# Moving masks, state updates and copies among the steps of a fused attention and feed-forward kernel

## The chip, the cores and the metric

The kernel runs on one core of one Trainium2 chip. The metric is the device time of one execution, in microseconds (us). The engines are TensorE (PE, matmuls; PEld is its weight load), VectorE (DVE), ScalarE (ACT), GpSimd (POOL) and SyncE (SP, which issues the DMAs here). Each engine works through its own list of instructions in the order written and waits for others on semaphores.

## The reference

The input goes through decaying linear attention, and the result through a feed-forward layer with a squared ReLU:

```python
for b in range(nb):                                   # blocks of 64 positions
    intra = np.einsum('bhic,bhjc->bhij', qb, kb) * Dmask[None]
    intra = np.einsum('bhij,bhjd->bhid', intra, vb)
    inter = np.einsum('bhid,bhde->bhie', qb * lam_pow[None], kv_state)
    out[:, :, sl] = intra + inter
    kv_state = lam_block[None, :, None, None] * kv_state + np.einsum('bhsd,bhse->bhde', kb_dec, vb)
x = attn.transpose(0, 2, 1, 3).reshape(B * S, H * D)  # 3072 tokens x 512
h = x @ w_in                                          # 512 x 2048
r = np.maximum(h, 0.0)
return (r * r) @ w_out                                # 2048 x 512
```

Batch 4, 8 heads, 768 positions, head size 64, all in float32.

## The kernel before

Tokens are cut into 24 chunks t of 128 (six per batch entry), each of two blocks of 64. Four chunks make a slice m of 512 tokens, so there are six slices. The feed-forward layer is done per slice in 16 steps f of 128 hidden features: `hidden(m, f)` makes h in PSUM by 12 matmuls of 512 columns (weights and inputs are split into a high and a low part, `wh`/`wl` and `xh`/`xl`, and three products are added), ACT takes the ReLU (`positive`) and squares it twice (`gh`, then h itself), DVE makes the low part (`rest`, tile `gl`), and `project` adds 12 more matmuls into four accumulators. PE's order is: hidden of step f, then the projection of step f-1.

The change lies in the loop of slice 0 (`m == 0`), the first of these passes. Three other things are done beside its 16 steps.

*Weights.* The weights come in as raw words in NLOT = 17 pieces u. Step f works on u = f + 2. `wload` sends for the raw words by DMA, `first` on ACT takes the absolute value (L210, tile A) and scales the low word (L215), DVE does `clamp` (L223), `shift` (L227), `sign` (L234) and `rounded` (L240), ACT writes `wh` by `upper` (L246) and DVE `wl` by `lower` (L249). Step f's hidden needs piece f. There are two A tiles, so `first` of piece u waits for `lower` of piece u-2. POOL's `turn` (L256) follows each `lower`. Below, clamp(3) means the clamp of piece 3.

*Attention of slice 1.* Chunks 4 to 7 are worked on here, and chunk 8 is begun. In steps 2, 6, 10 and 14 (`step == 2`) PE does a `burst` behind hidden: the scores of chunk t+1, the result of chunk t, and the key-value products ("news") of t+1, all in 64x64 matmuls (L386). It uses a PSUM tile y from the pool of h (two tiles, taken in turn) and two banks `b` from the pool `ps_b`. `keep` copies the result out (`xh`, `xl`; L454, L300), `masked` multiplies the scores by the decay mask into tile a (L484; for chunk 4, whose scores come from `look`, L477). The state is carried by `fade(t, b)`, which writes fd times the state before to the state behind, on ACT, four instructions (L514), and `advance(t, b)`, which adds the news of block b to it on DVE (L300, tile st). So advance(t, 0) needs fade(t, 0), and fade(t, 1) reads the state that advance(t, 0) wrote. POOL makes `prep_k` (L471) and `prep_q` (L466, tile qs), ACT the copies `copy_qx` (L169) and `copy_vx` (L164).

*Banks.* Chunk 4's scores and news are made by `look` at the end of step 0, in the two-bank tile `att` of the pool `ps_a`. At the start of step 2 `middle.close()` gives up that pool, and `ps_b` is opened on the same side of PSUM, so its two banks are the ones that `att` had. The framework lets the first matmul into them wait for the last reader of `att`.

The order of each engine's list is the order in which Python calls these functions; there is no scheduler. SP's DMAs too are issued in the order written, and one that waits for a buffer holds up those behind it.

Of the kernel before, what the change touches and what calls it, by code (L numbers as in the profile page):

```python
# [26 lines left out]
G = 4  # L27
# [15 lines left out]
def body(ctx: ExitStack, tc: tile.TileContext, qT, kT, kvq, lam, w, out):  # L43
# [118 lines left out]
    def copy_vx(t):  # L162
        for y, r in enumerate(rows):
            nc.scalar.copy(chunk[t]["vx"][r], chunk[t]["v"][rows[1 - y], 2 * y : 2 * y + 2])  # L164
# [16 lines left out]
    def pieces(u):  # L181
        return slice(max(2 * u - 1, 0), min(2 * u + 1, 2 * NF))
# [3 lines left out]
    def wload(u):  # L186
        nonlocal hole
        if u < NLOT:
            x = pieces(u)
            n = (x.stop - x.start) * DM  # L190
            if u and u % 3 == 0:
                raw[u] = sets[1]
            elif u == 0:
                x_ = wk.tile([P, 2 * DM], I64, name="raw", tag="raw")
                raw[u] = x_[:, 0:DM]
                hole = x_[:, DM : 2 * DM].bitcast(F32)
            else:
                raw[u] = wk.tile([P, n], I64, name="raw", tag="raw")
            for i, j in enumerate(range(x.start, x.stop)):
                of = (1, j // 2 - 1) if j and j % 2 == 0 else (1, NF - 1) if j == 2 * NF - 1 else (0, (j + 1) // 2)  # L200
                nc.sync.dma_start(out=raw[u][:, i * DM : (i + 1) * DM], in_=w[of[0], :, of[1]])
# [43 lines left out]
    def upper(u):  # L245
        nc.scalar.copy(flat(wh, u), cv[u][2].bitcast(F32))  # L246
# [59 lines left out]
    b_, t_, u_, c_, d_, af = (sq[:, i, 0 : NS - 1] for i in range(6))  # L306
# [166 lines left out]
    def masked(t):  # L473
        a = a_of[t] = a_last[0] if t >= G else wk.tile([P, 2, 2, 2, L], F32, name="a", tag="a")
        x, w_ = sc_of.pop(t), mask.rearrange("p j a i -> p j (a i)")
        if t <= G:
            V.tensor_tensor(  # L477
                out=a.rearrange("p j b a i -> p j b (a i)"),
                in0=x.rearrange("p j (b n) -> p j b n", b=2),
                in1=w_.unsqueeze(2).broadcast_to([P, 2, 2, 2 * L]), op=ALU.mult,  # L480
            )
            return
        for j in range(2):
            V.tensor_tensor(  # L484
                out=a[:, j].rearrange("p b a i -> p b (a i)"),
                in0=x[j].rearrange("p (b n) -> p b n", b=2),
                in1=w_[:, j].unsqueeze(1).broadcast_to([P, 2, 2 * L]), op=ALU.mult,
            )

    def before_block(n):  # L490
        return st[:, n % 3]
# [17 lines left out]
    def fade(t, b):  # L509
        n = 2 * t + b  # L510
        if n % (2 * NCB) and b < len(u_of[t]):
            old, new = (before_block(k).rearrange("p a j d -> p (a j) d") for k in (n, n + 1))
            for g in range(4):
                nc.scalar.activation(new[:, g], old[:, g], AF.Identity, scale=fd[:, g : g + 1])  # L514

    def advance(t, b):
        if b < len(u_of[t]):
            n = 2 * t + b
            new = before_block(n + 1).rearrange("p a j d -> p (a j d)")
            if n % (2 * NCB):  # L520
                add(new, u_of[t][b], new)
            else:
                V.tensor_copy(new, u_of[t][b])
        if b:
            del u_of[t]
# [67 lines left out]
    def positive(h):  # L593
        nc.scalar.activation(h, h, AF.Relu)  # L594
# [207 lines left out]
    def new_x(m):  # L802
        xs_of[m] = [wk.tile([P, KT, N], F32R, name=n, tag=n) for n in ("xh", "xl")]
# [98 lines left out]
    for m in range(PLAIN):  # L902
        if m == 0:
            new_x(1)
        else:
            held += [
                wk.tile([P, KT, N], F32, name=f"held{k}", tag=n) for k, n in enumerate(("xh", "xl"))
            ]
        for f in range(NF):
            h = hidden(m, f, *xs_of[m])  # L910
            if m == 0:
                t = G + f // 4
                step = f % 4
                u_ = f + 2
                if step == 2:
                    if f == 2:
                        middle.close()
                        ps_b = ctx.enter_context(
                            tc.tile_pool(name="ps_b", bufs=1, side="right", space=PSUM)
                        )  # L920
                    upper(u_ - 1)
                    x = burst(t + 1, True, True, lambda: positive(h))
                if f == 1:
                    load_kq(t + 1)
                    load_v(t + 1)
                if f == 1:
                    masked(t)
                    advance(t, 0)
                if u_ < NLOT:
                    if f:  # L930
                        clamp(u_)
                    if f == 1:
                        upper(u_ - 1)
                        lower(u_ - 1)
                    if f:
                        shift(u_)
                    sign(u_)
                if f > 1:
                    if step != 2:
                        upper(u_ - 1)  # L940
                    lower(u_ - 1)
                if f:
                    turn(u_ - 1)
                if step == 2:
                    prep_q(t + 1)
                    if t + 1 < 2 * G:
                        load_vx(t + 1)
                    load_kq(t + 2)
                    load_v(t + 2)
                    if t + 1 == 2 * G:  # L950
                        load_kq(t + 3)
                if f == 1:
                    fade(t, 1)
                    advance(t, 1)
                if step == 3:
                    fade(t + 1, 0)
                    masked(t + 1)
                    advance(t + 1, 0)
                if step == 0 and f:
                    fade(t, 1)  # L960
                    advance(t, 1)
                if f == 0:
                    positive(h)
                if f == 0 or step == 2:
                    rest(m, f, h, square(h))
                if u_ < NLOT:
                    rounded(u_)
                    wload(u_ + 3)
                if step == 1 or f == NF - 1:
                    prep_k(t + 1 if step == 1 else t + 2)  # L970
                if f and step != 2:
                    positive(h)
                    rest(m, f, h, square(h))
                if f == 1:
                    copy_qx(t)
                if step == 2:
                    keep(t, x)
                    if t + 1 == 2 * G:
                        copy_vx(t + 1)
                    copy_qx(t + 1)  # L980
                if f == NF - 1:
                    fade(t + 1, 1)
                    advance(t + 1, 1)
                if u_ + 1 < NLOT:
                    first(u_ + 1)
                if prev is not None:
                    project(*prev)
                if f == 0:
                    look(t)
                    fade(t, 0)  # L990
            else:
                t = 2 * G + 1 + f
                if f < 2 * G:
                    x = burst(t, True, True, lambda: positive(h))
                    rest(m, f, h, square(h))
                    keep(t - 1, x)
                    masked(t)
                    state(t)
                    if t + 1 < SOLO:
                        load_v(t + 1)  # L1000
                    prep_q(t)
                    if t + 2 < SOLO:
                        load_kq(t + 2)
                    if t + 1 < SOLO:
                        prep_k(t + 1)
                    copy_vx(t)
                else:
                    squared(m, f, h)
                if f - 1 in SUMS:
                    w_parts(SUMS.index(f - 1), S)  # L1010
                if f in SUMS:
                    S = w_sums(SUMS.index(f))
                if f < 2 * G:
                    copy_qx(t)
                if f == 2 * G + 1:
                    fetch(0)
                    fetch(1)
                if f > 2 * G:
                    x_sums(f - 2 * G - 1)
                    x_parts(f - 2 * G - 1)  # L1020
                project(*prev)
            prev = (m, f)
# [4 lines left out]
    for d in range((NM - PLAIN) // 2):  # L1027
        m1, m2 = PLAIN + 2 * d, PLAIN + 2 * d + 1
        last = d == (NM - PLAIN) // 2 - 1
        for i in range(NPAIR):  # L1030
            t = (PLAIN + 2) * G + i
# [93 lines left out]
```

## Time and profile before

| | us |
|---|---|
| runs, median of 3 (lowest to highest) | 589.23 (588.75 to 589.60) |
| the profiled execution | 588.08 |
| its span, first to last instruction | 586.2 |
| PE busy | 572.8 |
| DVE busy | 323.1 |
| ACT busy | 317.5 |

The profiled execution took 588.08 us, of which the span is 586.2; 1.9 us lie around it. A row of the time lines further below reads: start in us, length in us, engine, line, operation, tile written and tiles read, shapes, count of instructions merged, and in brackets the idle time of the engine just before with what ended it. A length of several merged instructions runs from the first start to the last end, and neighbours on one engine overlap by about 0.1 us. The pass over slice 0 runs from 26 to 130 us.

### The profile page before, as it was taken

Reading aid. Unit: us, or ns where it says so; the run is one execution under the profiler, and the core shown is the slowest. Engines: PE = TensorE matmul, PEld = TensorE weight load, DVE = VectorE, ACT = ScalarE, POOL = GpSimd, SP = SyncE. Lnnn points to the kernel's source line nnn. Section 1 sums busy time; section 2 is a strip of 40 time slices with the busy share of each in tenths; the row PEclk is TensorE's granted clock in tenths of the full one; section 3 lists DMA queues with packets and bytes.
Section 4 is the critical chain, followed back from the end, with each engine's and each line's share of the span. In section 5 each row is a group of like instructions: output and inputs, shape, how many; then the busy total and the mean of one; then the engine's idle time right before and its main releaser. Section 6 shows DMA issues by size and latency. Waiting matters only on the chain.

```text
span 586.2 us, 12793 instructions
## 1 busy us (share of the span) xinstructions
PE 572.8 (98%) x5240; PEld 470.1 (80%) x5240; DVE 323.1 (55%) x587; ACT 317.5 (54%) x594; POOL 66.7 (11%) x87
## 2 busy tenths in 40 slices
PE   8899999999999999999999999999999999999997
PEld 5777887788888888888888888888888888888885
DVE  6899999975767776534344343446433333334222
ACT  3698887976665465445545445634344444444221
POOL 7401202033232000011111101000000000000000
PEclk8999999999999999999999999999999999999999
DMA  8676667346797933856554553300354444411001
GB/s 335 220 283 228 223 217 229 104 128 196 243 364 260 348 130 103 284 164 197 168 166 137 179 173 98 126 1 0 102 168 126 125 122 120 122 50 73 1 0 72
DMA packets 52089, 93.62 MB, mean 160 GB/s; under 512 B 4672, under 2 KB 19520, under 8 KB 52032
## 3 DMA queue, kind: packets, MB, share of 16 engines
q1 hardware_dynamic: 52032, 92.82, 49.5%
q8 instruction: 41, 0.67, 0.4%
q14 instruction: 16, 0.13, 0.1%
HBM read 71.83 MB, written 20.97 MB: 158 GB/s over the span
## 4 chain that ended last, share of the span: by engine, by line
PE 87%; DVE 6%; ACT 3%; issue 2%; DMA 1%; POOL 1%; POOLq 0%; DVEq 0%
PE h L729 26%; PE acc L623 14%; PE acc L628 14%; PE acc L624 13%; PE h L587 11%; PE h L386 4%; PE b L386 3%; DVE A L234 1%; PE att L79 1%; DVE wl L249 1%; DVE A L240 1%; ACT A L210 1%; DVE A L227 1%; DVE A L223 1%; DVE st L500 1%
## 5 line engine op out<-in xcount | busy, mean ns | idle before, releaser
L623 PE MATMUL acc<-wh,gh 128*128 128x512 f32 x384 | 151.7, 395 | 0.0
L624 PE MATMUL acc<-wl,gh 128*128 128x512 f32 x384 | 149.6, 389 | 0.0
L628 PE MATMUL acc<-wh,gl 128*128 128x512 f32 x384 | 149.3, 390 | 0.1
L623 PEld LDWEIGHTS acc<-wh,gh 128*128 128x128 f32 x384 | 72.1, 188 | 16.0 <-issue 0.3
L628 PEld LDWEIGHTS acc<-wh,gl 128*128 128x128 f32 x384 | 72.1, 188 | 15.2
L624 PEld LDWEIGHTS acc<-wl,gh 128*128 128x128 f32 x384 | 72.1, 188 | 14.4
L608 DVE TENSOR_TENSOR gl<-h,gh 128x512 fp32r<-128x512 f32 x48 | 33.1, 689 | 69.7 <-ACT h L603 69.7
L594 ACT ACTIVATE h<-h 128x512 f32<-128x512 f32 x48 | 28.1, 584 | 69.7 <-PE h L587 36.0
L300 DVE TENSOR_TENSOR temp<-h,temp 128x512 f32<-128x512 f32 x48 | 33.0, 688 | 56.9 <-PE h L729 46.8
L729 PE MATMUL h<-wh,ring 128*128 128x512 f32 x224 | 60.0, 390 | 0.0
L594 ACT ACTIVATE temp<-temp 128x512 f32<-128x512 f32 x16 | 10.1, 632 | 88.6 <-DVE temp L300 88.6
L729 PEld LDWEIGHTS h<-wh,ring 128*128 128x128 f32 x224 | 42.0, 188 | 8.9 <-DVE r L300 0.3
L466 POOL TENSOR_TENSOR qs<-set,qpow 128x512 f32<-128x512 f32 (+1 forms) x21 | 26.5, 1260 | 170.7 <-PE b L386 159.2
L587 PE MATMUL h<-xh,wh 128*128 128x512 f32 x128 | 34.6, 392 | 3.0 <-DVE a L484 2.2
L300 DVE TENSOR_TENSOR r<-h,temp 128x512 f32<-128x512 f32 x24 | 16.6, 692 | 34.2 <-PE h L729 33.1
L608 DVE TENSOR_TENSOR gl<-r,gh 128x512 fp32r<-128x512 f32 x24 | 16.6, 690 | 32.9 <-ACT gh L761 32.9
L729 PE MATMUL h<-wl,ring 128*128 128x512 f32 x112 | 34.5, 389 | 0.0
L587 PE MATMUL h<-xh,wl 128*128 128x512 f32 x128 | 34.5, 391 | 0.0
L587 PE MATMUL h<-xl,wh 128*128 128x512 f32 x128 | 34.3, 389 | 0.0
L761 ACT CAST gh<-r 128x512 fp32r<-128x512 f32 x24 | 14.9, 621 | 30.0 <-PE acc L624 30.0
L587 PEld LDWEIGHTS h<-xh,wh 128*128 128x128 f32 x128 | 23.7, 188 | 9.0 <-ACT gh L598 3.0
L729 PE MATMUL h<-wh 128*128 128x512 f32 x112 | 30.1, 390 | 0.0
(180 smaller groups left out, 1040.1 us busy)
## 6 DMA issues: line engine op xcount, KB each, us to landing
ring<-wd SPq DMA_DIRECT2D x56, 256.0 KB, 2.9
raw<-in_w SPq DMA_DIRECT2D x22, 512.0 KB, 4.7
set<-in_kvq SPq DMA_DIRECT2D x19, 512.0 KB, 3.8
wd<-hl SPq DMA_DIRECT2D x16, 512.0 KB, 5.0
wh<-wd SPq DMA_DIRECT2D x28, 256.0 KB, 2.9
wl<-wd SPq DMA_DIRECT2D x28, 256.0 KB, 2.8
set<-in_kT SPq DMA_DIRECT2D x22, 256.0 KB, 4.2
set<-in_w SPq DMA_DIRECT2D x10, 512.0 KB, 4.9
```

Of the source, the lines that this page charges most:

```text
L79: nc.tensor.matmul(w_[:, 0], st[:, 0, 0].rearrange("p a b -> p (a b)"), st[:, 0:2].rearrange("p n c a b -> p (n c a b)"), start=True, stop ...
L300: lambda o, x, y, op=op: V.tensor_tensor(out=o, in0=x, in1=y, op=op)
L386: nc.tensor.matmul(self.banks[row][rows[col], at : at + D], lhsT, rhs, start=key not in self.begun, stop=stop, skip_group_check=True,)
L466: nc.gpsimd.tensor_tensor(out=z, in0=x, in1=w_, op=ALU.mult)
L587: nc.tensor.matmul(h, wt[:, w_in(f), kt * P : (kt + 1) * P], x[:, kt], start=k == 0, stop=k == 11)
L594: nc.scalar.activation(h, h, AF.Relu)
L608: V.tensor_tensor(out=gl, in0=r, in1=gh.bitcast(F32), op=ALU.subtract)
L623: nc.tensor.matmul(accs[m][i], gh[:, cs], wh[:, j], start=f == 0, stop=False)
L624: nc.tensor.matmul(accs[m][i], gh[:, cs], wl[:, j], start=False, stop=False)
L628: nc.tensor.matmul(accs[m][i], gl[:, cs], wh[:, j], start=False, stop=end)
L729: nc.tensor.matmul(bank, w[:, kw * HALF + kt * P : kw * HALF + (kt + 1) * P], x_slot(2 * c + kt, kx), start=first and q == 0, stop=q == 5, ...
L761: nc.scalar.copy(gh, r_of[f])
```

## The change

Five things are written elsewhere in the loop of slice 0. No instruction is added or removed.

- `masked(t+1)` moves from step 3 (behind `fade(t+1, 0)`) to step 2, right behind `keep`.
- At f == 1, `wload(5)` stands behind the loads of chunk 5; before it was called at the end of step 0, ahead of them.
- `advance(4, 0)` moves from behind `masked(4)` to just ahead of `fade(4, 1)`, and `advance(4, 1)` from f == 1 to f == 2.
- `copy_qx(t+1)` moves from step 2 to the end of step 3, `copy_vx(8)` from f == 14 to f == 15.

```diff
                 if f == 1:
                     load_kq(t + 1)
                     load_v(t + 1)
-                if f == 1:
+                    wload(u_ + 2)
                     masked(t)
-                    advance(t, 0)
...
                 if f == 1:
+                    advance(t, 0)
                     fade(t, 1)
+                if f == 2:
                     advance(t, 1)
                 if step == 3:
                     fade(t + 1, 0)
-                    masked(t + 1)
                     advance(t + 1, 0)
...
                     rounded(u_)
-                    wload(u_ + 3)
+                    if f:
+                        wload(u_ + 3)
...
                 if step == 2:
                     keep(t, x)
-                    if t + 1 == 2 * G:
-                        copy_vx(t + 1)
+                    masked(t + 1)
+                if step == 3:
                     copy_qx(t + 1)
                 if f == NF - 1:
+                    copy_vx(t + 1)
                     fade(t + 1, 1)
                     advance(t + 1, 1)
```

DVE's list at the start of step 1, before (-) and now (+). `att` is the tile of `look`, `a<-att,mask` is `masked(4)`, `st<-att,st` an advance of chunk 4, L223 a clamp, L249 the `lower` and L240 the `rounded` of a weight piece:

```order
 L240 ISA A<-raw,A 128x2048
 L477 TENSOR_TENSOR a<-att,mask 128x512
-L300 TENSOR_TENSOR st<-att,st 128x256
 L223 TENSOR_SCALAR A<-A 128x1024
 L249 TENSOR_TENSOR wl<-A,wh 128x1024
```

An advance has left the place behind the mask. The other one of step 1, behind `sign(3)`, is untouched in the list but is now block 0's instead of block 1's. DVE's list in step 2, where `gl<-h,gh` is the low part of h and `xl` that of `keep`:

```order
 L234 SCALAR_TENSOR_TENSOR A<-raw,A 128x1024
 L249 TENSOR_TENSOR wl<-A,wh 128x1024
+L300 TENSOR_TENSOR st<-att,st 128x256
 L608 TENSOR_TENSOR gl<-h,gh 128x512
 L240 ISA A<-raw,A 128x2048
 L300 TENSOR_TENSOR xl<-h,xh 128x2x128
```

Block 1's advance is the new row, behind `lower(3)` of step 2.

ACT's list in step 1 and the start of step 2 now (it has the same rows before, except that the third waits for an earlier DVE instruction and the last for one more). The first four-fold L514 is fade(4, 0), the next two rows fade(4, 1); `L246` is `upper`, `L594`, `L598` and `L603` are the ReLU and the squares of h, `L210` is the start of the next weight piece:

```order
L514 ACTIVATE st<-st,fd 128x64 x4
L246 CAST wh<-A 128x1024 [waits DVE_49]
L514 ACTIVATE st<-st,fd 128x64 [waits DVE_49,Activation_49]
L514 ACTIVATE st<-st,fd 128x64 [waits Activation_49] x3
L594 ACTIVATE h<-h 128x512 [waits PE_49]
L598 ACTIVATE gh<-h 128x512 [waits Activation_49]
L603 ACTIVATE h<-h 128x512
L169 COPY qx<-qs 64x256 [waits Pool_49]
L169 COPY qx<-qs 64x256
L210 ACTIVATE A<-raw 128x1024 [waits DMAHW5_49,DMAHW4_49]
```

No row of these moved; what moved is the DVE instruction for which the third row, the start of fade(4, 1), waits: advance(4, 0).

PE's list at the burst of step 2, before:

```order
L587 MATMUL h<-xh,wl 128x512 x3
L587 MATMUL h<-xl,wh 128x512 x4
L386 MATMUL h<-set_92 64x64 [waits DMAHW1_49,DMAHW0_49,DVE_49]
L386 MATMUL b_777<-set_92 64x64 [waits PE_49]
L386 MATMUL h<-set_92 64x64
```

and now:

```order
L587 MATMUL h<-xh,wl 128x512 x3
L587 MATMUL h<-xl,wh 128x512 x4
L386 MATMUL h<-set_92 64x64 [waits DMAHW7_49,DMAHW6_49,DVE_49]
L386 MATMUL b_776<-set_92 64x64 [waits DVE_49,PE_49]
L386 MATMUL h<-set_92 64x64
```

The order of the matmuls is the same; the first one into a `b` bank has a wait for DVE that it did not have. The banks are those of `att`, and the last reader of `att` is now advance(4, 1), which stands in step 2.

## Rows read from the trace of the kernel before

**Rows 1.** The page's first part: engine, busy us (share of the span), instructions.

```profile
span 586.2 us, 12793 instructions
PE 572.8 (98%) x5240; PEld 470.1 (80%) x5240; DVE 323.1 (55%) x587; ACT 317.5 (54%) x594; POOL 66.7 (11%) x87
```

**Rows 2.** Busy time of each engine in a stretch of the pass over slice 0: stretch, then PE, PEld, DVE, ACT and POOL busy us (instructions), granted clock of PE, DMA share, GB/s.

```profile
60.00:80.00 20.00, 20.00 (x207) 16.39 (x205) 19.70 (x24) 16.25 (x26) 4.10 (x6) 1.00 0.67 219
```

**Rows 3.** Who waited for whom in the stretch 24 to 130 us: us in total, times, longest us.

```profile
ACT qx L169 <- POOL qs L466: 6.2, 4, 2.0
...
DVE A L223 <- ACT A L210: 0.8, 3, 0.3
```

**Rows 4.** PE's time line: the starts of the burst of step 2 and of the projection behind it, the first and the last hidden matmuls of step 3, and the first of steps 4, 5, 6 and 12.

```profile
43.88 0.27 PE L386 MATMUL h<-set 64*64 64x64 f32 x1 [1.32 <-DVE gl L608]
...
45.90 0.50 PE L623 MATMUL acc<-wh,gh 128*128 128x512 f32 x1
...
48.77 1.07 PE L587 MATMUL h<-xh,wh 128*128 128x512 f32 x4
...
50.81 0.84 PE L587 MATMUL h<-xl,wh 128*128 128x512 f32 x3
...
55.77 1.15 PE L587 MATMUL h<-xh,wh 128*128 128x512 f32 x4 [1.40 <-DVE a L484]
...
61.29 1.07 PE L587 MATMUL h<-xh,wh 128*128 128x512 f32 x4
...
66.73 1.07 PE L587 MATMUL h<-xh,wh 128*128 128x512 f32 x4
...
105.76 1.17 PE L587 MATMUL h<-xh,wh 128*128 128x512 f32 x4 [0.84 <-DVE a L484]
```

**Rows 5.** DVE's time line in step 1: mask of chunk 4, its two additions to the state (37.67 and 41.67), the weight pieces 2 and 3 between them, gl of step 1, and `clamp(4)`, the first of step 2.

```profile
36.35 0.68 DVE L477 TENSOR_TENSOR a<-att,mask 128x512 f32<-128x512 f32 x1
37.67 0.42 DVE L300 TENSOR_TENSOR st<-att,st 128x256 f32<-128x256 f32 x1 [0.63 <-ACT st L514]
38.01 0.68 DVE L223 TENSOR_SCALAR A<-A 128x1024 f32<-128x1024 f32 x1
38.61 1.23 DVE L249 TENSOR_TENSOR wl<-A,wh 128x1024 fp32r<-128x1024 f32 x1
39.75 0.69 DVE L227 TENSOR_SCALAR A<-A 128x1024 uint32<-128x1024 uint32 x1
40.53 1.22 DVE L234 SCALAR_TENSOR_TENSOR A<-set,A 128x1024 uint32<-128x1024 uint32 x1
41.67 0.41 DVE L300 TENSOR_TENSOR st<-att,st 128x256 f32<-128x256 f32 x1
...
43.14 0.68 DVE L608 TENSOR_TENSOR gl<-h,gh 128x512 fp32r<-128x512 f32 x1
43.74 1.01 DVE L223 TENSOR_SCALAR A<-A 128x1024 f32<-128x1024 f32 x1
```

**Rows 6.** ACT's time line in step 1: `upper(2)`, fade(4, 1), the ReLU of h of step 1, the copy of qx, `first(4)` and `upper(3)`.

```profile
37.53 1.05 ACT L246 CAST wh<-A 128x1024 fp32r<-128x1024 f32 x1
38.47 1.08 ACT L514 ACTIVATE st<-st,fd 128x64 f32<-128x64 f32 x4
39.43 0.59 ACT L594 ACTIVATE h<-h 128x512 f32<-128x512 f32 x1
...
40.55 0.59 ACT L603 ACTIVATE h<-h 128x512 f32<-128x512 f32 x1
41.17 0.83 ACT L169 COPY qx<-qs 64x256 f32<-64x256 f32 x2
42.03 1.15 ACT L210 ACTIVATE A<-raw 128x1024 f32<-128x1024 f32 x1
...
44.10 1.03 ACT L246 CAST wh<-A 128x1024 fp32r<-128x1024 f32 x1
```

**Rows 7.** DVE's time line of a plain step (4): `clamp(6)` and, three instructions on, `lower(5)`; and `lower(14)` of step 13 with the PE matmuls of step 14 that read its `wl`.

```profile
57.93 0.69 DVE L223 TENSOR_SCALAR A<-A 128x1024 f32<-128x1024 f32 x1
...
60.52 1.22 DVE L249 TENSOR_TENSOR wl<-A,wh 128x1024 fp32r<-128x1024 f32 x1
...
116.31 1.22 DVE L249 TENSOR_TENSOR wl<-A,wh 128x1024 fp32r<-128x1024 f32 x1
...
117.67 1.11 PE L587 MATMUL h<-xh,wl 128*128 128x512 f32 x4
```

**Rows 8.** The granted clock: four stretches as in rows 2 (the clock is the last column but two; 1.00 is 2.4 GHz, 0.50 is 1.2 GHz), the last matmuls of the program, and the same 27 narrow matmuls of the opening at the lower and at the higher clock.

```profile
10.60:14.00 3.40, 2.92 (x90) 2.78 (x86) 1.63 (x5) 1.94 (x8) 3.20 (x4) 0.50 1.02 419
14.00:17.42 3.42, 2.97 (x107) 2.81 (x105) 2.45 (x12) 2.11 (x7) 3.42 (x4) 0.50 0.82 330
17.42:20.85 3.43, 2.82 (x151) 2.41 (x143) 2.62 (x10) 3.32 (x7) 0.85 (x1) 1.00 0.80 274
...
584.05:586.20 2.15, 0.00 (x0) 0.00 (x0) 0.00 (x0) 0.00 (x0) 0.00 (x0) 0.50 0.27 102
...
581.38 0.61 PE L628 MATMUL acc<-wh,gl 128*128 128x512 f32 x2
...
12.18 1.02 PE L386 MATMUL h<-set 64*64 64x64 f32 x27 [0.48 <-DVE mask L355]
...
21.73 0.63 PE L386 MATMUL h<-lent 64*64 64x64 f32 x27 [0.38 <-DVE st L500]
```

## The prediction

> **What bounds the kernel now.** The page's first part comes first [rows 1]: PE is busy for 572.8 of 586.2 us, so an end moves only when PE idles more or less. The table by stretches [rows 2] says why PE idles at all in the pass over slice 0: in 20 us there DVE works 19.70 us and PE 20.00, while ACT works 16.25 and POOL 4.10. Two engines are full at once, and either one's delay is soon the other's. The waits [rows 3] show the only gaps in DVE's chain that belong to this change: ACT waits 6.2 us in four places for POOL's qs before it copies qx, and DVE then waits for A behind it, three times, 0.3 us at most. PE's time line [rows 4] shows what the masks cost: step 4 begins 1.40 us late and step 12 0.84 us late, each waiting for a L484, because the PSUM tile of the burst is not free until its scores are masked. These 2.2 us are what the change can win at most by its first part. Then I read DVE's and ACT's lists in step 1 [rows 5, 6], since that is where the two additions to the state were moved.
>
> **Masks and copies.** `masked(t+1)` goes ahead of clamp, shift, sign and lower, so PE's 1.40 and 0.84 us go; but the two L484 (about 0.34 us each from start to start) now stand ahead of `lower`, so wl of the next step comes 0.7 us later, and DVE, which is full, sets the pace: nothing is won unless DVE idles less. That it does: with `copy_qx` out of step 2, `first` no longer stands behind POOL's qs. Of the three waits of DVE for A in rows 3, one of 0.3 us lies in step 11 and is won; a smaller gap in step 7 I put at 0.1 us, an estimate. Together 0.4 us. `copy_qx` and `copy_vx` are the same instructions on ACT in another place; beyond step 2 ACT has 3.75 us of idle time in 20 [rows 2], which hides them, except in step 3 (below). `wload(5)` behind the loads of chunk 5 waits for the same buffer as before (free once `rounded(2)` ends, just ahead of the mask at 36.35 [rows 5]), and chunk 5 comes sooner on SP. I cost this at nothing: raw piece 5 is first read behind the burst of step 2, at 43.88 at the earliest, and by the sum below far later, so a microsecond more on SP's queue would not be seen.
>
> **The first hold-up: fade(4, 1).** Before, advance(4, 0) runs at 37.67, right behind the mask, and fade(4, 1) starts on ACT at 38.47 as soon as `upper(2)` lets it [rows 5, 6]. Now the DVE list is mask, clamp(3), lower(2), shift(3), sign(3), advance(4, 0). DVE gains nothing by the addition that left: lower(2) needs `upper(2)`, which ends at 37.53 + 1.05 = 38.58, so it starts at 38.6 as before and the addition stands at 41.67, where the other one stood, and ends at 42.08. fade(4, 1) reads what it writes, so it starts at 42.12 instead of 38.47, 3.65 us later, and ACT's list behind it waits: ReLU and squares of step 1, copy_qx(4), first(4). From fade's start to ACT's ReLU are 0.96 us, to the end of the last square 40.55 + 0.59 - 38.47 = 2.67, to first(4) 3.56, to `upper(3)` 5.63 [rows 6]. Hence the square ends at 44.79, gl of step 1 runs on DVE at 44.83 instead of 43.14 and ends at 45.51, A(4) is there at 42.12 + 3.56 + 1.15 = 46.83.
>
> **The second hold-up: the banks of `att`.** The burst of step 2 writes the banks that `att` held, and the last reader of `att` is now advance(4, 1), which stands in DVE's list behind lower(3) of step 2. That addition needs A(4): clamp(4) at 46.87, lower(3) 2.59 us behind it (57.93 to 60.52 in a plain step [rows 7]) at 49.46, the next instruction 1.14 us on (38.61 to 39.75 [rows 5]) at 50.60, its end 0.41 later at 51.01. PE's first burst matmul into a bank follows at 51.07 (0.06 us, as from 43.82 to 43.88 [rows 4, 5]) instead of 43.88: **7.19 us later**. Queued behind it on PE are the whole burst, the projection of step 1 and hidden of step 3; ACT's `mark` and the squares of step 2 wait for the burst's scores.
>
> **The clock.** PE has then idled since hidden of step 2 ended, at 43.88 - 1.32 = 42.56 [rows 4], for 8.5 us but for one narrow matmul. In this trace the granted clock fell to 0.50 at 584.05, 2.06 us after the last matmuls ended (581.38 + 0.61), and in the opening it was at 0.50 from 10.60 to 17.42, while only narrow matmuls ran, and at 1.00 behind them [rows 8]. So I expect the burst to start at 1.2 GHz. At that clock 27 narrow matmuls took 1.02 us, against 0.63 at the higher [rows 8], 1.62 times; the burst's 45.90 - 43.88 = 2.02 us become 3.27, 1.25 more. If the lower clock lasts through the burst alone, that is all; if it lasts 6.8 us from the burst's start (as the opening's low stretch, 10.60 to 17.42), the 3.55 us behind the burst are wide matmuls at half speed and cost 1.78 more, 3.03 in all; if it doesn't fall, nothing. I take 1.6, near the first (the burst and 0.7 us behind it, which costs 0.35), since the row at 14.00 to 17.42 shows that work much like the burst was followed by the higher clock. The Trainium skill (TensorE: Matmul & The Clock Gate, "HAM oscillation — how this bites in real kernels") tells of a kernel whose matmul groups each start at half the clock because PE idles for a transfer between them; this trace agrees in its last rows, where PE's idling ends at 0.50. By that rule alone the sum would be the one below, and a clock that holds would contradict it.
>
> **The sum.** Hidden of step 3 starts 48.77 - 43.88 = 4.89 us behind the burst's start, plus 1.6: at 57.56 instead of 48.77. Its h is done 50.81 + 0.84 - 48.77 = 2.88 us on, at 60.44. ACT then needs 41.17 - 39.43 = 1.74 us for ReLU and squares, 0.86 for the qx that now stands there, and 1.15 for A(6), with 0.04 us of handing over on either side [rows 6]: clamp(6) at 64.27, against 57.93 [rows 7]. That is 6.3 us. From here on DVE is full as before, does the same work to lower(14), and gains the 0.4 us of the copies, so lower(14) ends 5.9 us later than 116.31 + 1.22 = 117.53. PE's step 14 took its wl at 117.67 before, right behind it, and does so again (PE alone would be there sooner: from 57.56 on, eleven steps of 66.73 - 61.29 = 5.44 us and two bursts of 2.02 [rows 4] end at 121.4, while step 14 then starts at 117.67 - 0.91 + 5.9 = 122.7, with the four matmuls ahead of the wl ones at 5.44/24 us each). Behind step 14 DVE has little to do and PE never waits, so the 5.9 us stay to the end. The profiled execution took 588.08; with 5.9 it is 594.0. That execution lies 1.15 us below the median of the runs shown, so on the median I forecast 589.23 + 5.9 = **595.1 us**.
>
> **Rivals** (times on the median).
> - *The clock holds at 2.4 GHz* (its price is then 0 instead of 1.6). For it: PE idled at 1.00 too, as for 0.38 us ahead of the matmuls at 21.73 [rows 8], and 1.32 us ahead of this very burst [rows 4], and the clock stayed. Against it: this gap is eight us long. Step 3 starts at 55.96, clamp(6) 4.7 us late, less 0.4: +4.3, 593.5.
> - *The banks don't hold the burst* (second hold-up absent, first one there). Then the burst starts at 45.57, behind gl of step 1; hidden of step 3 waits for gl of step 2, which stands behind advance(4, 1) and ends at about 51.6; DVE is 2.4 us late at clamp(6): +2.0, 591.2. Against it: the list of PE now has the wait for DVE at exactly that matmul.
> - *The lower clock lasts longer than the opening's*, by 4 us, which costs 2 more than the 3.03: 1.25 + 1.78 + 2 in place of the 1.6, so +9.3, 598.5. For it: in the opening the first low row, 90 narrow matmuls, was not followed by the higher clock [rows 8]. Against it: behind this burst come wide matmuls without a pause.
> - *Not slower: ACT is not held at fade(4, 1)*, and the other addition is early too, so that the burst starts as before. It decides whether ACT's ReLU of step 1 still starts near 39.4. Then DVE's wait for A in step 3 goes as well (0.3 us [rows 3]), the 0.4 us stay, and clamp(4), 1.01 us at 43.74 against 0.69 in a plain step [rows 5, 7] and then beside a POOL instruction that now comes sooner, gives 0.3: -1.0, 588.2, not slower. Against it: fade(4, 1) reads the state that advance(4, 0) writes, whatever the order.
>
> **Chances and range.** The forecast has 0.65, the clock that holds 0.14, the longer low clock 0.11, banks that don't hold 0.05, ACT not held 0.03; 0.02 is left for a gain that I don't see. No change, as far as a measurement of this kernel can tell, is within 0.2%, 1.2 us; the case of ACT not held lies inside it, the first four on the slow side. So faster 0.02, same 0.03, slower 0.95. The range takes in the clock's two ends (+4.3 to +7.3, 593.5 to 596.5) and at the top half of the way to the longer case, at the bottom 0.5 us for the runs' own spread: 593.0 to 597.5.
>
> **What the changed profile would show.** fade(4, 1) on ACT near 42 us, waiting for DVE st L300; gl of step 1 near 44.8; PE with a wait of 5 us or more ahead of its first burst matmul into b in step 2, put down to DVE st L300, and the burst near 51; PEclk at a half in the slice about 44 to 55; no wait of PE for a L484 in steps 4 and 12, but some for wl L249; no wait of ACT for qs behind the burst. The forecast is wrong if the burst of step 2 starts before 46, or if step 14's lag behind before is less than half of step 4's, in which case PE and DVE have more slack than rows 2 say.

## The result and the profile after

The changed kernel takes 595.97 us (median of 4 runs, 595.29 to 597.13), the kernel before 588.99 us (4 runs, 588.63 to 589.60). The ratio is 1.0119, with a 95% interval of 1.0099 to 1.0140: 7.0 us slower, where the forecast was 5.9 slower. The profiled execution took 597.13 us, of which the span is 595.3.

The page's first part of the kernel after, as [rows 1]:

```profile
span 595.3 us, 12795 instructions
PE 575.9 (97%) x5240; PEld 473.2 (79%) x5240; DVE 323.7 (54%) x587; ACT 318.3 (53%) x594; POOL 67.2 (11%) x87
```

The span grew by 9.1 us and PE's busy time by 3.1. (The two instructions more are in none of these engines' counts.) So 6 us are new idle time of PE, and 3.1 us went into the same 5240 matmuls: some of them ran slower. The waits in the stretch 24 to 130 us, in the columns of [rows 3], say what PE idled for:

```profile
PE b L386 <- DVE st L300: 5.2, 1, 5.2
...
ACT st L514 <- DVE st L300: 4.4, 1, 4.4
DVE gl L608 <- ACT h L603: 4.3, 2, 2.6
...
PE h L386 <- DVE gl L608: 3.9, 1, 3.9
```

The first two were not there before. Both are waits for an addition to the state: the second is fade(4, 1) behind advance(4, 0), the first is the burst behind advance(4, 1). PE's old wait for a L484 (1.40 and 0.84 in [rows 4]) and ACT's for qs [rows 3] are gone: the change does what it says in those places.

The same instants as in [rows 4 to 7] in the kernel after, first on DVE (the mask of chunk 4, lower(2), sign(3), advance(4, 0), gl of step 1, clamp(4), advance(4, 1), clamp(6), lower(14)):

```profile
37.52 0.68 DVE L477 TENSOR_TENSOR a<-att,mask 128x512 f32<-128x512 f32 x1
...
39.78 1.23 DVE L249 TENSOR_TENSOR wl<-A,wh 128x1024 fp32r<-128x1024 f32 x1 [0.97 <-ACT wh L246]
...
41.70 2.04 DVE L234 SCALAR_TENSOR_TENSOR A<-set,A 128x1024 uint32<-128x1024 uint32 x1
43.66 0.41 DVE L300 TENSOR_TENSOR st<-att,st 128x256 f32<-128x256 f32 x1
...
46.94 0.69 DVE L608 TENSOR_TENSOR gl<-h,gh 128x512 fp32r<-128x512 f32 x1 [1.73 <-ACT h L603]
48.87 0.69 DVE L223 TENSOR_SCALAR A<-A 128x1024 f32<-128x1024 f32 x1 [1.24 <-ACT A L210]
...
52.60 0.42 DVE L300 TENSOR_TENSOR st<-att,st 128x256 f32<-128x256 f32 x1
...
66.94 0.69 DVE L223 TENSOR_SCALAR A<-A 128x1024 f32<-128x1024 f32 x1 [1.27 <-ACT A L210]
...
124.73 1.22 DVE L249 TENSOR_TENSOR wl<-A,wh 128x1024 fp32r<-128x1024 f32 x1
```

then fade(4, 1) on ACT, POOL's prep_k of chunk 5 beside sign(3), and on PE the first score of chunk 5, the first matmul into a `b` bank, the first of the projection behind the burst, and the first of hidden of step 3:

```profile
44.17 1.07 ACT L514 ACTIVATE st<-st,fd 128x64 f32<-128x64 f32 x4 [4.42 <-DVE st L300]
...
41.61 1.05 POOL L471 TENSOR_TENSOR set<-set,near 128x512 f32<-128x512 f32 x1
...
47.68 0.33 PE L386 MATMUL h<-set 64*64 64x64 f32 x2 [3.88 <-DVE gl L608]
53.16 0.34 PE L386 MATMUL b<-set 64*64 64x64 f32 x1 [5.16 <-DVE st L300]
...
56.78 0.79 PE L623 MATMUL acc<-wh,gh 128*128 128x512 f32 x1
...
60.30 1.07 PE L587 MATMUL h<-xh,wh 128*128 128x512 f32 x4
```

The mask itself stands 1.17 us later than before (37.52 against 36.35), ahead of everything that the change touches on DVE: ACT began on raw piece 2 that much later, when its DMA had landed (before in the first fence, after in the second).

```profile
29.81 1.17 ACT L210 ACTIVATE A<-raw 128x1024 f32<-128x1024 f32 x1 [2.69 <-DMA raw<-in_w]
```

```profile
31.00 1.15 ACT L210 ACTIVATE A<-raw 128x1024 f32<-128x1024 f32 x1 [2.35 <-DMA raw<-in_w]
```

In the twelve profiles of this study the mask starts anywhere from 36.14 to 38.94 us, so I count from it. The table gives each start as the distance from the mask, worked out from these rows and [rows 4 to 7]:

| start | before | after | later by | forecast |
|---|---|---|---|---|
| sign(3) | 4.18 | 4.18 | 0 | 0 |
| advance(4, 0) | (other block's) 5.32 | 6.14 | 0.82 | 0 |
| fade(4, 1) | 2.12 | 6.65 | 4.53 | 3.65 |
| gl of step 1 | 6.79 | 9.42 | 2.63 | 1.69 |
| the burst (after: into `b`) | 7.53 | 15.64 | 8.11 | 7.19 |
| hidden of step 3 | 12.42 | 22.78 | 10.36 | 8.8 |
| clamp(6) | 21.58 | 29.42 | 7.84 | 6.3 |
| lower(14) | 79.96 | 87.21 | 7.25 | 5.9 |

The chain is the forecast one, link by link. Two links are longer than forecast. The first is in the second row: sign(3) starts on time but takes 2.04 us instead of 1.22, and the addition behind it, fade(4, 1) and the burst all inherit the 0.82. The second is from the burst to step 3: 60.30 - 53.16 = 7.14 us against 4.89, so 2.25 for the clock instead of 1.6: the burst took 3.62 us instead of 2.02 [rows 4], and the projection behind it 3.52 instead of 2.87. The clock after, in the columns of [rows 2] (granted clock last but two):

```profile
27.47:47.95 20.48, 16.43 (x130) 13.07 (x130) 16.38 (x19) 13.57 (x25) 1.58 (x2) 1.00 0.77 266
47.95:58.19 10.24, 5.08 (x114) 4.69 (x114) 6.64 (x7) 6.23 (x10) 1.44 (x2) 0.50 0.22 82
58.19:62.00 3.81, 3.81 (x18) 3.12 (x17) 3.74 (x8) 3.07 (x7) 0.00 (x0) 1.00 0.93 284
```

PE's clock was at 1.2 GHz from 47.95 to 58.19, through the burst and the first 1.4 us of the projection behind it. Between step 3 and lower(14), 3.11 us are won back: 2.52 up to clamp(6), where the forecast had 8.8 - 6.3 = 2.5, and 0.60 behind it, where it had 0.4.

Of the 9.05 us between the two profiled executions 1.17 therefore lie ahead of the mask, 7.25 in the pass over slice 0, and 0.6 later (two waits of PE there read "issue", 0.7 us in all, 0.2 before). The 7.25 lie close to the 7.0 us of the medians.

### The profile page after: what moved, and what is told of

Its sections match the earlier page's. It is cut to its first block, busy times and chain, and to the rows that moved or that the text cites. A ratio compares the mean times of both kernels' runs of the same rounds, so it can differ in the third digit from the quotient of the medians.

```text
span 595.3 us, 12795 instructions
## 1 busy us (share of the span) xinstructions
PE 575.9 (97%) x5240; PEld 473.2 (79%) x5240; DVE 323.7 (54%) x587; ACT 318.3 (53%) x594; POOL 67.2 (11%) x87
## 4 chain that ended last, share of the span: by engine, by line
PE 87%; issue 4%; DVE 3%; DMA 3%; POOL 1%; SPq 1%; ACT 1%; POOLq 0%; ACTq 0%
PE h L729 26%; PE acc L623 15%; PE acc L628 14%; PE acc L624 14%; PE h L587 12%; PE h L386 4%; PE b L386 3%; DMA lent<-in_kvq 2%; DMA set<-in_kvq 1%; DVE A L234 1%; DVE wl L249 1%; POOL qs L466 0%; SPq L134 0%; DVE A L240 0%; DVE A L227 0%
## 5 line engine op out<-in xcount | busy, mean ns | idle before, releaser
L594 ACT ACTIVATE h<-h 128x512 f32<-128x512 f32 x48 | 27.9, 582 | 72.9 <-PE h L587 39.0
L300 DVE TENSOR_TENSOR temp<-h,temp 128x512 f32<-128x512 f32 x48 | 33.0, 688 | 57.3 <-PE h L729 47.2
L594 ACT ACTIVATE temp<-temp 128x512 f32<-128x512 f32 x16 | 10.1, 632 | 88.8 <-DVE temp L300 88.8
L300 DVE TENSOR_TENSOR r<-h,temp 128x512 f32<-128x512 f32 x24 | 16.6, 692 | 34.4 <-PE h L729 33.2
L729 PE MATMUL h<-wh,wl 128*128 128x512 f32 x112 | 30.0, 389 | 0.0
```

The source lines that it names most:

```text
L300: lambda o, x, y, op=op: V.tensor_tensor(out=o, in0=x, in1=y, op=op)
L729: nc.tensor.matmul(bank, w[:, kw * HALF + kt * P : kw * HALF + (kt + 1) * P], x_slot(2 * c + kt, kx), start=first and q == 0, stop=q == 5, ...
```

## Experiments

My theory: the two advances alone make the kernel slower, through two waits in a row, and the clock that falls in them adds about a third; the load that was moved costs 0.8 by way of POOL; masks and copies gain a little. The rivals: the masks cost DVE time that PE waits for later; either advance alone does the harm; the clock costs nothing, since other engines set the pace.

**Both advances put back** into the changed kernel, all else as changed:

```diff
                     masked(t)
+                    advance(t, 0)
...
-                    advance(t, 0)
                     fade(t, 1)
-                if f == 2:
                     advance(t, 1)
```

> The change with both advances of chunk 4 back where they were (masks, loads and copies stay moved). Theory (the two advances make the whole loss): 588 to 589.5 us against 589.0 before, the burst of step 2 starts within 1 us of the kernel before. Rival (masks ahead of the weight work, or the copies in step 3, cost the time): 593 or more.

588.00 us against 588.48, ratio 0.9985 (0.9969 to 1.0000). The whole loss goes with the advances; what is left of the change is worth a small gain at most. Its burst starts at

```profile
45.31 0.27 PE L386 MATMUL h<-set 64*64 64x64 f32 x1 [2.16 <-DVE gl L608]
```

which is 8.32 us behind the mask, 0.79 more than before, since sign(3) takes 2.04 us here too. The clock fell behind it (last section), and step 3 comes 6.41 us behind the first matmul into `b` instead of 4.89. Yet lower(14), counted from the mask, comes 0.53 us sooner than before. Here DVE sets the pace and does not wait for the late step, so the low clock costs nothing that can be seen at lower(14).

**One advance at a time.** The first of these kernels moves only advance(4, 0) to its late place, the second only advance(4, 1):

```diff
                     fade(t, 1)
-                if f == 2:
                     advance(t, 1)
```

> The change with advance(4, 1) back in step 1, behind fade(4, 1); advance(4, 0) stays late. Theory: fade(4, 1) still waits about 4.4 us on ACT, but the burst is no longer held by a st L300; it starts right behind gl of step 1. +2 to +3, 591 to 592. Rival (all of the loss comes through ACT's wait, the bank wait is only where it shows): 595 to 596.

```diff
                     masked(t)
+                    advance(t, 0)
...
-                    advance(t, 0)
                     fade(t, 1)
```

> The change with advance(4, 0) back behind masked(4); advance(4, 1) stays in step 2. Theory: no wait of ACT at fade(4, 1), but the burst still waits for advance(4, 1), behind lower(3) of step 2, and starts near 48.7; PE's idle stretch is about 6 us, so the clock may fall or not: +2 if it holds (591), +4 if it falls (593). Rival (the bank wait costs nothing by itself): 588 to 589.5.

The first: 591.64 us, ratio 1.0043 (1.0029 to 1.0058), 3.2 us slower than before. The second: 592.75, 1.0058 (1.0035 to 1.0082), 4.3 slower. Each has its own wait and not the other's. But the load of raw piece 5 is still moved in both (sign(3) takes 2.04 us), and the clock fell in both (from the burst to step 3 it took 6.42 and 7.12 us), so these are not the prices of the waits alone. From the kernel with both advances put back each differs by one advance only; against it they are 3.6 and 4.8 us slower. With only advance(4, 0) late, ACT is held and the burst waits for gl of step 1, but not for an addition (ACT's and PE's time lines):

```profile
43.91 1.06 ACT L514 ACTIVATE st<-st,fd 128x64 f32<-128x64 f32 x4 [4.42 <-DVE st L300]
...
47.41 0.27 PE L386 MATMUL h<-set 64*64 64x64 f32 x1 [3.92 <-DVE gl L608]
47.42 0.27 PE L386 MATMUL b<-set 64*64 64x64 f32 x1
```

With only advance(4, 1) late, ACT is not held, and the bank holds the burst (waits, columns of [rows 3]):

```profile
PE b L386 <- DVE st L300: 3.8, 1, 3.8
...
PE h L386 <- DVE gl L608: 1.9, 1, 1.9
```

So each delay exists without the other. They are in series: the wait for the bank shrinks from 5.2 to 3.8 us when ACT's list is not held, because advance(4, 1) stands behind A(4), which that list makes.

**The advances alone**, moved in the kernel before, against **masks and copies without them**:

```diff
-                    advance(t, 0)
...
                 if f == 1:
+                    advance(t, 0)
                     fade(t, 1)
+                if f == 2:
                     advance(t, 1)
```

> The kernel before with only the two advances moved as in the change. Theory: the whole loss is here, +6 to +8: 594.5 to 596.5; burst of step 2 held by st L300. Rival (part of the loss needs the masks, copies or loads as well): below 593.

The second is the changed kernel with the advances and `wload(5)` as before:

```diff
-                    wload(u_ + 2)
                     masked(t)
+                    advance(t, 0)
...
-                    advance(t, 0)
                     fade(t, 1)
-                if f == 2:
                     advance(t, 1)
...
-                    if f:
-                        wload(u_ + 3)
+                    wload(u_ + 3)
```

> Masks and copies moved, advances and wload(5) as before. Theory: DVE idles 0.7 us less (0.3 in step 3, 0.4 later) and no more than before otherwise, so -0.4 to -1.2 us: 587.3 to 588.1 against 588.5. Rival (masks ahead of the weight work cost as much as the copies win): 588.3 to 589.

The advances alone: 594.92 us against 589.26, ratio 1.0095 (1.0073 to 1.0118), 5.7 us slower. In this kernel sign(3) has its old length (1.23 us), so it is the cleanest test of the forecast's core. DVE's mask, sign(3), advance(4, 1), clamp(6) and lower(14), then PE's first burst matmul into `b` and the first row of step 3:

```profile
36.78 0.69 DVE L477 TENSOR_TENSOR a<-att,mask 128x512 f32<-128x512 f32 x1
...
40.92 1.23 DVE L234 SCALAR_TENSOR_TENSOR A<-set,A 128x1024 uint32<-128x1024 uint32 x1
...
51.00 0.42 DVE L300 TENSOR_TENSOR st<-att,st 128x256 f32<-128x256 f32 x1
...
64.40 0.69 DVE L223 TENSOR_SCALAR A<-A 128x1024 f32<-128x1024 f32 x1
...
122.75 1.22 DVE L249 TENSOR_TENSOR wl<-A,wh 128x1024 fp32r<-128x1024 f32 x1
...
51.57 0.33 PE L386 MATMUL b<-set 64*64 64x64 f32 x1 [5.15 <-DVE st L300]
...
57.78 1.07 PE L587 MATMUL h<-xh,wh 128*128 128x512 f32 x4
```

Advance(4, 1) stands 14.22 us behind the mask; the forecast had 50.60 - 36.35 = 14.25. From the burst (51.57) to step 3 (57.78) it was 6.21 us, 1.32 more than before, and clamp(6) is 64.40 - 36.78 - 21.58 = 6.04 us late where the forecast, with 1.6 for the clock, had 6.3. At lower(14) it is 6.01 us late: from clamp(6) on nothing is won back here, where masks and copies stand in their old places.

Masks and copies alone: 587.97 us, ratio 0.9975 (0.9964 to 0.9987), 1.3 us faster than before, a little more than the 0.4 to 1.2 expected.

**The load of raw piece 5 put back** to the end of step 0:

```diff
-                    wload(u_ + 2)
                     masked(t)
...
-                    if f:
-                        wload(u_ + 3)
+                    wload(u_ + 3)
```

> The change with wload(5) back at the end of step 0. Theory: POOL's prep_k(5) then runs later, no longer beside sign(3), which takes 1.22 us again instead of 2.04, so advance(4, 0) and all behind it come 0.8 us sooner: 594.7 to 595.7. Rival (the order of the loads costs nothing): sign(3) stays at 2.0 or the time stays at 596.

595.74 us against 589.26, ratio 1.0103 (1.0080 to 1.0126). By time alone this doesn't tell: its 6.5 us over before lie inside the interval of the change's 7.0. The traces do tell. First prep_k of chunk 5 before the change, on POOL:

```profile
43.15 1.06 POOL L471 TENSOR_TENSOR set<-set,near 128x512 f32<-128x512 f32 x1 [2.67 <-DMA set<-in_kvq]
```

and now the mask, sign(3), prep_k and the burst with the load put back:

```profile
37.59 0.68 DVE L477 TENSOR_TENSOR a<-att,mask 128x512 f32<-128x512 f32 x1
...
41.82 1.23 DVE L234 SCALAR_TENSOR_TENSOR A<-set,A 128x1024 uint32<-128x1024 uint32 x1
...
44.25 1.18 POOL L471 TENSOR_TENSOR set<-set,near 128x512 f32<-128x512 f32 x1 [2.48 <-DMA set<-in_kvq]
...
52.47 0.34 PE L386 MATMUL b<-set 64*64 64x64 f32 x1 [5.16 <-DVE st L300]
```

With raw piece 5 sent for first, chunk 5 lands later, POOL's prep_k starts at 44.25 when sign(3) is done, and sign(3) takes 1.23 us. The burst stands at 14.88 us behind the mask instead of 15.64, and lower(14) is 6.54 us late instead of 7.25. So the order of two loads on SP's queue set the length of a DVE instruction, by setting when POOL runs; in the six kernels here with the load moved sign(3) takes 2.04 or 2.05 us, in the six without 1.22 or 1.23.

This kernel differs from the one with the advances alone by masks and copies only, and it is not faster: 595.74 against 594.92 us, with intervals that overlap. Masks and copies win 0.58 us behind clamp(6) here (7.12 to 6.54), but from the burst to step 3 it took 7.17 us instead of 6.21. So a gain by masks and copies on the whole, beside late advances, is not shown.

**PE kept busy in the gap.** `hidden` of step 2 already has 6 idle matmuls ahead of it (into h, which the real ones then overwrite). I raised their number to 36, and then to 48:

```diff
-        for _ in range({1: 10, 2: 6}.get(f, 0) if m == 0 else 0):
+        for _ in range({1: 10, 2: 36}.get(f, 0) if m == 0 else 0):
```

> The change with 30 more idle matmuls ahead of hidden of step 2 (36 instead of 6; their result is overwritten), so that PE works until about 50.5 while it would wait. Theory (clock costs about 2 us of the 7): the clock stays at 2.4 GHz over the burst, which still starts near 52; 593.5 to 594.5. Rival (the low clock is most of the loss): below 591. Rival (the clock costs nothing, because PE is not the pace there): 595.5 to 596.5, with the clock high.

> The change with 42 more idle matmuls ahead of hidden of step 2, so that PE does wide matmuls until the burst may start. Theory: the clock stays at 2.4 GHz, and from the first burst matmul into b to hidden of step 3 it takes 4.9 to 5.2 us as before instead of 7.1: 593.5 to 594.5. Rival (the clock falls all the same, or its cost is hidden): 595.5 or more.

With 36: 596.57 us (594.1 to 598.98), ratio 1.0123 (1.0083 to 1.0164). This missed its aim and the 593.5 to 594.5 expected: PE still idled 2.40 us ahead of the burst, and the clock fell behind it (first fence, with the granted clock last but two). The four runs lie far apart, and in the profiled one, the slowest, the mask itself stands 2.59 us later than before; counted from it lower(14) is 6.50 us late. With 48: 593.92 us, 1.0086 (1.0059 to 1.0113), and the clock did not fall there (second fence).

```profile
54.58 0.24 PE L386 MATMUL b<-set 64*64 64x64 f32 x1 [2.40 <-DVE st L300]
...
54.94:58.36 3.42, 3.42 (x102) 3.30 (x95) 1.59 (x2) 1.94 (x6) 1.02 (x1) 0.50 0.11 30
```

```profile
36.42 0.69 DVE L477 TENSOR_TENSOR a<-att,mask 128x512 f32<-128x512 f32 x1
...
51.52 0.42 DVE L300 TENSOR_TENSOR st<-att,st 128x256 f32<-128x256 f32 x1
...
52.20:57.10 4.90, 4.90 (x125) 4.32 (x125) 2.82 (x5) 4.67 (x9) 1.29 (x1) 1.00 0.19 41
57.11 1.07 PE L587 MATMUL h<-xh,wh 128*128 128x512 f32 x4
...
121.60 1.22 DVE L249 TENSOR_TENSOR wl<-A,wh 128x1024 fp32r<-128x1024 f32 x1
```

With 48, advance(4, 1) still runs 15.1 us behind the mask (51.52 - 36.42; 15.08 in the changed kernel), and the burst begins behind it and the last idle matmuls at 52.23, 15.81 us behind the mask. But step 3 comes 4.88 us behind the burst, as before the change (4.89). So the hold-ups stay and the clock's share goes: lower(14) is 5.22 us later than before instead of 7.25, 2.0 us less (2.25 for the clock, less 0.17 by which the burst is later). The medians, 4.7 us over before against 7.0, agree in size, though their intervals overlap.

**Masks alone and copies alone**, moved in the kernel before:

```diff
                 if step == 3:
                     fade(t + 1, 0)
-                    masked(t + 1)
...
                     keep(t, x)
+                    masked(t + 1)
```

> The kernel before with only masked(t+1) moved behind keep. Theory (DVE is full, so nothing is won unless it idles less): PE no longer waits for a L484 in steps 4 and 12 but for a wl L249 instead, and the time stays within 0.5 us of before. Rival (the masks alone make the gain of masks and copies together): -1 to -1.6 us.

```diff
-                    if t + 1 == 2 * G:
-                        copy_vx(t + 1)
+                if step == 3:
                     copy_qx(t + 1)
                 if f == NF - 1:
+                    copy_vx(t + 1)
```

> The kernel before with only copy_qx and copy_vx moved. Theory: ACT no longer waits for qs ahead of the weight work of steps 2, 6, 10, 14, DVE's waits for A of 0.3 us go, PE's waits for L484 stay but come sooner: -0.4 to -0.8 us. Rival (no gain without the masks, whose wait ends last on PE): -0.2 to +0.2.

587.48 us against 588.97 for the masks, ratio 0.9970 (0.9957 to 0.9983); 587.95 for the copies, 0.9976 (0.9964 to 0.9989). Each alone wins about as much as both together, 1.0 to 1.5 us by the medians; counted from the mask, lower(14) comes 1.08 (masks), 1.01 (copies) and 1.06 us (both) sooner. For the masks I had expected no change beyond 0.5 us, and the rival was right; the copies won more than the 0.4 to 0.8 expected. With the masks moved, DVE in step 3 reads:

```profile
53.12 0.41 DVE L484 TENSOR_TENSOR a<-h,mask 128x256 f32<-128x256 f32 x1
53.45 0.41 DVE L484 TENSOR_TENSOR a<-b,mask 128x256 f32<-128x256 f32 x1
53.78 0.68 DVE L223 TENSOR_SCALAR A<-A 128x1024 f32<-128x1024 f32 x1
```

and in the kernel before the same clamp reads

```profile
51.47 0.70 DVE L223 TENSOR_SCALAR A<-A 128x1024 f32<-128x1024 f32 x1 [0.29 <-ACT A L210]
```

DVE used to idle here until ACT had made A behind qx. With the masks in that place it has work while ACT copies, and no idle time is left. The copies, moved away, remove the same idle time from the other side. That is why the two gains don't add: from the mask to lower(14) DVE's rows leave 2.24 us idle before, and 1.57 (masks), 1.61 (copies) and 1.53 us (both) in these kernels. The gap shrinks by 0.6 to 0.7 us; the rest of the 1.0 us was not taken apart. ACT's wait for qs stays with the masks moved (6.1 us) and costs nothing. The best kernel of the study is one of these three, about 0.25 to 0.3% faster than before; their intervals don't separate them.

## Why the prediction was right

The direction, the place and the mechanism were right, and the measured 595.97 lies 0.9 us above the forecast 595.1. The steps:

- *The first hold-up* is there as worked out: fade(4, 1) waits 4.42 us for DVE st L300, and the kernel in which only advance(4, 0) is late shows it without the other (3.6 us slower than with both put back).
- *The second hold-up* is there too, at the very matmul that the order named, which waits 5.2 us for advance(4, 1). With sign(3) at its old length the sum for that addition came out at 14.25 against 14.22 us. The rival in which the banks don't hold is refuted by that wait, and the one in which ACT is not held by fade(4, 1)'s.
- *The load that I cost at nothing* was the most mis-sized term: it made sign(3) 0.82 us longer, and putting it back brings the burst 0.76 us and lower(14) 0.71 us sooner. I asked only when raw piece 5 is needed and wrote that a microsecond on SP's queue would not be seen. I noted that chunk 5 comes sooner, but did not follow what then starts sooner: prep_k on POOL, onto sign(3), which stands on the path that holds ACT and PE. I did name such an overlap in the rival in which ACT is not held, but for clamp(4), as a gain; prep_k had been beside clamp(4) before (1.01 us against 0.69 in [rows 5, 7]), and by coming sooner it met sign(3).
- *The clock*: it fell, as expected, and cost 2.25 us in this trace against 1.6, between the burst alone (1.25) and the far end (3.03). The burst lost 1.60 us where the factor 1.62 from [rows 8] had given 1.25, and the projection 0.65 where I had put 0.35. This is one execution, the slowest of the four. The kernel with 48 idle matmuls shows that about 2 us of it reach lower(14). The rival of a longer low clock (5.03 for the clock) is refuted by the 2.25. The rival in which it holds would have been 2 us better than what happened; what each stretch at 1.2 GHz lasted differed, 10.24 us here and 6.83 in the kernel with the advances alone (47.74 to 54.57), and why stays open.
- *Masks and copies*: 0.60 us behind step 3 against 0.4, right in size. One step of the working was wrong: it let the copies alone make DVE idle less. The masks do so too, by filling the wait for A; without the hold-ups the gain is 1.0 to 1.5 us, which I had not foreseen. And of the three waits for A in [rows 3], which it put behind qx, one (0.19 us, in step 0) lies ahead of the mask.
- *DVE's pace to lower(14)*: held. The delay at clamp(6) came through to lower(14) less the gain, and to the end of the pass unchanged; in the kernel with the advances alone, which has no such gain, 6.04 us at clamp(6) are 6.01 at lower(14). PE had no slack, as [rows 2] said.

The terms as measured close: 7.19 + 0.82 + 0.1 to the burst, 2.25 for the clock, less 2.52 and 0.60, is 7.24 us, and 7.25 is what the trace shows at lower(14). The forecast is 1.1 us short of the measured 7.0 because its two largest errors, the load and the clock, point the same way; none was hidden by another.

## What to carry to other kernels

When a reader of a PSUM tile is moved later, look up which tile gets those banks next: the wait appears on the first writer of another tile, and in this kernel it held PE for 5.2 us with a 0.4-us addition. When a DMA is moved, price not only the transfer that comes later but the engine work that the other one releases sooner, and what runs beside it on DVE. Before giving an instruction a place, look for an idle gap on its engine that another engine's work already makes: the masks fitted into one and won 1.5 us.

## What the runs showed of the hardware

A POOL operation can stretch a DVE operation beside it by most of its own length. Sign(3) took 2.04 us beside a prep_k of 1.05 and 1.23 without; in the changed kernel `rounded(4)` took 2.31 us beside prep_q of 1.27, and 2.12 us at that place before, against 1.22 for the same form with no POOL operation beside it:

```profile
56.24 2.31 DVE L240 CUSTOM_DVE_ANT_0 A<-raw,A 128x2048 uint16<-128x2048 uint16 x1
...
56.20 1.27 POOL L466 TENSOR_TENSOR qs<-set,qpow 128x512 f32<-128x512 f32 x1 [3.21 <-PE b L386]
```

The added 0.81 and 1.09 us are 77% and 86% of the POOL operations. Not every DVE operation is stretched: gl of step 1, which reads h from PSUM and gh, took 0.68 us at 43.14 before the change [rows 5] with prep_k beside it from 43.15 on, and 0.69 us with no POOL operation beside it in the kernel after (at 46.94). The Trainium skill (SBUF — State Buffer, "SBUF: two separate sides") says that the two engines share a port pair under an exclusive lock, which one instruction holds for its whole length, and counts a VectorE operation with two SBUF inputs among those that meet it, against a GpSimd operation that reads SBUF; this trace agrees. By that rule sign(3), which reads two SBUF tiles and starts 0.09 us behind prep_k, would wait out the rest of it, an estimate of 0.96 us; the row says 0.81.

The clock fell in places where PE had not idled for long. In the kernel with both advances put back, PE idled 2.16 us ahead of the burst, ran narrow matmuls at 1.00, and the granted clock then fell (stretches, granted clock last but two):

```profile
43.00:46.69 3.69, 1.53 (x93) 1.38 (x96) 3.62 (x7) 3.64 (x6) 0.00 (x0) 1.00 0.27 44
46.69:50.10 3.41, 3.41 (x40) 2.85 (x30) 3.41 (x4) 2.58 (x6) 0.98 (x2) 0.50 0.78 300
```

In the kernel with 36 idle matmuls PE waited 2.40 us, and the clock was at 0.50 from 54.94 to 58.36. Before the change, 1.32 us at the same place [rows 4] were followed by 1.00 throughout. The three kernels that win (masks, copies, or both) wait 1.3 us there too. Whether the wait or the narrow matmuls behind it decide was not tried apart.
